# Attention and two feed-forward layers on one core: 288 bytes of padding, a shorter warm-up, and the odd slices of the last matmul tile by tile

## The chip, the cores and the metric

The kernel runs on one core of one Trainium2 chip. The metric is the device time of one execution in microseconds. [...]

## The reference

```python
scores = scale * np.matmul(q, k.transpose(0, 1, 3, 2))       # batch 4, heads 8, seq 576, head_dim 64
thresh = np.max(scores, axis=-1, keepdims=True) - tau
scores = np.where(scores >= thresh, scores, -1000000000.0)
scores = scores - np.max(scores, axis=-1, keepdims=True)
attn = np.exp(scores)
attn = attn / (np.sum(attn, axis=-1, keepdims=True) + 1e-09)
attn_out = np.matmul(attn, v)
x = np.ascontiguousarray(attn_out.transpose(0, 2, 1, 3)).reshape(B * S, H * D)   # 2304 x 512
h = x @ w_in                                                 # layer 1: 512 -> 2048
g = np.where(h >= 1, h, np.where(h <= -1, 0.0, (h + 1) ** 2 / 4))
x = g @ w_out                                                # 2048 -> 512
h = x @ w2_in                                                # layer 2: 512 -> 2048
r = np.maximum(h, 0.0)
out = (s * (r * r) + b) @ w2_out                             # 2304 x 512
```

## The kernel before

**A planner writes the order.** Every piece of work is handed to a list (`add`) with the engines that may do it, an estimate for each, a priority, and the data that it reads and writes. `Sched.run` then plays the list through in a model of its own and fixes the order on every engine; the program is issued in that order. So one changed piece can shift the order everywhere behind it. Where the model sees TensorE without work, it puts in a filler: a product of the identity matrix with itself into a free PSUM bank, which nobody reads (`fill`, L1397).

**Stages.** Attention comes first, head by head: scores on TensorE (L576 and L585), their minimum on VectorE (L631), the exponential on ScalarE (L634), the masking with the sum on VectorE (L639), normalising (L669, L674), transposes on TensorE (L695, L711), the product with the values (L733, L734). In its gaps, TensorE does the first eight of layer 1's sixteen slices of 128 hidden columns (L928, L961). Then follow three passes (`PASSES`): the rest of layer 1, and layer 2 in two halves of eight slices. Each pass takes three blocks of 768 tokens; in each block `gemm1` (L1223) makes eight slices of the hidden layer with seven products for each pair of slices, and a second matmul sums them with the output weights. An operand is kept as two float32r parts, high and low, so that a product is made of three matmuls: high times high, high times low, low times high.

**Layer 2's second matmul** (`gemm2`, L1299). A block has six tiles of 128 tokens, each with its own PSUM bank. The loaded operand is a slice of the hidden layer for 128 tokens (`G_b`), the streamed one 512 columns of output weights (`P.unit`). `rows` lists the slices in the order in which they get ready: 0, 2, 4, 6 (even), then 1, 3, 5, 7 (odd). When a bank is complete, VectorE adds it to the sum of the earlier pass (`joined`, L1131), or an engine copies it (`copied`), and SyncE's queue stores the tile (L1318).

**Where operands lie.** `lr` and `lh` are allocated from the left of a partition's bytes: `lr` starts at byte 17088, `lh` at 122560. The pools of the right side end at the top of the partition; the last of them, `final`, holds `pr` (starting at byte 163808) and behind it `pf`. `G_b` lies in `pr`, each slice 6144 bytes and its low part 3072 behind the high one, a tile's 128 columns every 512 bytes. The 44 units of weights, 2048 bytes each, lie in `lr` (36), `lh` (3) and `pr` (5, the low part of slice 3 and both parts of slices 5 and 7). Two of the slices, `G_b[5]` and `G_b[7]`, also take in turn the split input of the next block's `gemm1` (`ring`).

**The start.** `warm_up` makes the identity on GpSimd, copies it to `ident_r`, and issues 27 transposes of it on TensorE; the first heads' scores stand behind them in TensorE's order. The first operands `r0` to `r3` come by DMA and are scaled on ScalarE (L513) or GpSimd (L511) before the scores.

Of the kernel before, what the change touches and what calls it, by code (L numbers as in the profile page):

```python
# [7 lines left out]
F32 = mybir.dt.float32  # L8
# [24 lines left out]
NSX, NV = 4, 2  # L33

AHEAD = 1
WARM = 9

FILL = 200000.0
NE, NP, NST, NH, LEAD = 2, 3, 4, 3, 3
NYS = 8  # L40
CONV0 = 0.0
# [22 lines left out]
NJ = 4  # L64
# [19 lines left out]
O_EXTRA = 8 * BT * 2 * NJ  # L84
PR_BYTES = O_EXTRA + UNIT * (NPLACE - NLEFT - NTAIL - NFREE)
PF_BYTES = 8 * BT

# [35 lines left out]
class Sched:  # L125
# [72 lines left out]
    def run(self):  # L198
# [27 lines left out]
        while left:  # L226
# [22 lines left out]
            for e in engines:  # L249
# [51 lines left out]
                    break  # L301
                for item in held:
                    heapq.heappush(q, item)
                if e == "pe" and busy[e] <= now < self.fill_until:

                    b = next((b for b in self.fill_banks if bank_free.get(b, 0.0) <= now), None)
                    if b is not None:
                        t = Task()
                        t.alts, t.prio, t.idx, t.group, t.after = [], (9, 0), len(self.tasks) + seq, Group([(b,)]), 0.0
                        t.group.banks, t.group.left, t.succ, t.start = (b,), 1, [], now  # L310
                        t.fn = ("pe", self.fill_ns, self.fill(b))
                        bank_free[b] = HELD
                        busy[e] = array.run(now, self.fill_ns + self.CHANGE.get((self.kind, None), 0))
                        self.kind = None
                        self.burst = 0
                        order.append(t)
                        seq += 1
                        heapq.heappush(events, (busy[e], seq, t))
# [47 lines left out]
def attention_then_ffn(tc, qk, v, tau, w1, w2, s2, b2, out):  # L366
# [51 lines left out]
    garr = [xp_.tile([128, 2 * TM], F32R, name=f"g{i}") for i in range(NGL)]  # L418
    at_cm = tc.tile_pool(name="attn", bufs=1, side="right")
    ap_ = at_cm.__enter__()  # L420
    ident_r = ap_.tile([128, 128], F32R, name="identr")
    hs_b = [Buf("LF", 1280 * i, TM) for i in range(NH)]
    c_b = [Buf("LF", 3840 + 1280 * i, TM) for i in range(NH)]
    ye_b = [Buf("LF", 7680 + 1280 * i, TM) for i in range(2)]
# [39 lines left out]

    def consts():
        make_identity(nc, ident)
        nc.gpsimd.tensor_copy(out=ident_r, in_=ident)
        for c, x in ((half, 0.5), (part_c, 1.0 / S), (tiny_c, 1e-9)):
            nc.vector.memset(c, x)

# [304 lines left out]
    def warm_up():  # L775

        g = Group([(7,)])

        def mm():
            for _ in range(3 * WARM):  # L780
                nc.tensor.transpose(bank[7][:, 0:128].bitcast(F32R), ident_r, ident_r)

        add([("pool", 1260.0, consts)], (0, 0), w=["ident"])
        add([("pe", WARM * 213.0, mm)], (0, 0), r=["ident"], w=[("bank", g)], group=g)

# [23 lines left out]
    def final():  # L809
        late["md"].__exit__(None, None, None)  # L810
        xg.__exit__(None, None, None)
        late["cm"] = tc.tile_pool(name="final", bufs=1, side="right")
        q = late["cm"].__enter__()
        arena["PR"] = q.tile([128, PR_BYTES // 4], F32R, name="pr")
        arena["PF"] = q.tile([128, PF_BYTES // 4], F32, name="pf")

    def after(tasks, fn, key, r=()):
        sw = add([("host", 1, fn)], (0, aidx[0] + 1), r=r, w=[key])
# [234 lines left out]
    class Pass:  # L1053
# [6 lines left out]
        def product(self, p, j):  # L1060
            return ORDER.index(p) * self.nj + j
# [218 lines left out]
    def gemm2(P, t0, T):  # L1280

        if P.layer == 1:
            return gemm2_across(P, t0, T)

        m, n = T // 128, 512
        prs = [fresh() for _ in range(m)]
        ny = 6 + 4 * P.last
        gy = [(Group(ANY8), y_b[turn("y", ny)]) for _ in range(m)]
        rows = P.rows()

        def tokens(i):
            return slice(t0 + 128 * i, t0 + 128 * i + 128)

        def mm(f, i, g):
            o = bank[g.banks[0]][:, 0:n]
            wh, wl = (P.unit[P.out(f, y)](0, 512) for y in range(2))
            gh, gl = G_b[f](128 * i, 128), G_b[f](BT + 128 * i, 128)
            for s, (a, y) in enumerate(((gh, wh), (gh, wl), (gl, wh))):
                nc.tensor.matmul(o, a, y, start=(f == rows[0] and s == 0), stop=(f == rows[-1] and s == 2))  # L1299

        def sums(i):
            if P.n > 1 and i < m:
                y = gy[i][1]
                add([("sp", DMA_ISSUE, lambda: nc.sync.dma_start(out=y(), in_=yD[tokens(i), :]))], (0, prs[i][1][1] - 16),
                    r=[("yd", t0, i)], w=y.keys(), lag=128 * 4 * n)

        for i in range(ny):
            sums(i)
        for f in rows:
            for i in range(m):  # L1310
                ku = P.unit[P.out(f, 0)].keys() + P.unit[P.out(f, 1)].keys()
                kg = G_b[f].keys(128 * i, 128) + G_b[f].keys(BT + 128 * i, 128)
                product(prs[i][0], 3 * mm_ns(n), lambda f=f, i=i: mm(f, i, gy[i][0]), ku + kg, gy[i][0])
        for i in range(m):
            g, y = gy[i]
            po = prs[i][2]
            (joined if P.n > 1 else copied)(g, n, y, y.keys(), po)
            add([("sp", DMA_ISSUE, lambda y=y, i=i: nc.sync.dma_start(out=(out if P.last else yD)[tokens(i), :], in_=y()))], po,  # L1318
                r=y.keys(), w=[] if P.last else [("yd", t0, i)], lag=128 * 4 * n)
            sums(i + ny)  # L1320
# [150 lines left out]
```

## Time and profile before

| | |
|---|---|
| median of 3 runs | 1083.65 us (1081.87 to 1083.82) |
| time of the profiled execution | 1079.24 us |
| span of its profile | 1077.4 us |
| TensorE busy | 1052.1 us, 98% of the span, 6491 records |
| VectorE, ScalarE, GpSimd busy | 802.2, 704.6, 428.3 us |
| granted clock, mean | 1.0 |

The span reaches from the first to the last instruction that the profiler saw; 1.8 us of the time lie around it. A busy TensorE is not one at its peak, since ends of matmuls are modelled: the pace is read from start to start. A float32 product of the identity is two records.

### The profile page before, as it was taken

What the parts mean: (1) busy time and instruction counts of PE and PEld (TensorE: products, weight loads), DVE (VectorE), ACT (ScalarE), POOL (GpSimd) and SP (SyncE); (2) the same over time, 40 slices, a digit from 0 to 9 for tenths busy, and PEclk for the clock granted to TensorE, in tenths of its full rate; (3) what the DMA queues carried; (4) which work ended last, traced back from release to release, by engine and by line L of the source; (5) the groups of instructions that cost most, each with busy time, mean ns of one, the idle gap of its engine ahead of it and who ended that gap; (6) DMA issues with size and microseconds to landing.
All of it is one profiled execution on the core that took longest, in us unless ns stands there. A gap on an engine that the chain in (4) does not pass through costs nothing.

```text
span 1077.4 us, 19033 instructions
## 1 busy us (share of the span) xinstructions
PE 1052.1 (98%) x6491; PEld 925.3 (86%) x6491; DVE 802.2 (74%) x1596; ACT 704.6 (65%) x1322; POOL 428.3 (40%) x653
## 2 busy tenths in 40 slices
PE   9989999999999999999999999999999999999998
PEld 6556877788888898899999999998989889898996
DVE  7988998797887899757888979786796726356372
ACT  7998888898998988734535446265684626346260
POOL 5766767889898978332302111120100101000000
PEclk9999999999999999999999999999999999999999
DMA  5654455565647665599856499843638951140112
GB/s 169 201 156 148 137 184 193 187 199 174 184 137 217 182 198 169 188 355 365 297 173 224 129 307 348 309 168 131 230 128 279 343 174 63 40 137 20 60 30 87
DMA packets 105120, 199.95 MB, mean 186 GB/s; under 512 B 11328, under 2 KB 33344, under 8 KB 105024
## 3 DMA queue, kind: packets, MB, share of 16 engines
q1 hardware_dynamic: 105024, 198.75, 55.9%
q8 instruction: 51, 0.84, 0.3%
q14 instruction: 45, 0.37, 0.1%
HBM read 134.61 MB, written 64.09 MB: 184 GB/s over the span
## 4 chain that ended last, share of the span: by engine, by line
PE 71%; ACT 8%; DVE 6%; issue 2%; POOL 2%; DMA 1%; DVEq 0%; ACTq 0%; POOLq 0%
PE ps L1223 23%; PE ps L1299 18%; PE ps L1263 9%; PE ps L928 5%; PE ps L961 4%; PE ps L695 2%; PE ps L733 2%; PE ps L1009 2%; PE ps L585 2%; ACT p L674 2%; DVE p L639 1%; ACT e L634 1%; ACT pt L687 1%; PE ps L576 1%; PE ps L734 1%
## 5 line engine op out<-in xcount | busy, mean ns | idle before, releaser
L1223 PE MATMUL ps<-pr,lr 128*128 128x384 f32 x816 | 144.7, 336 | 0.0
L1223 PEld LDWEIGHTS ps<-pr,lr 128*128 128x128 f32 x816 | 141.7, 188 | 0.4 <-DVE lg L1131 0.2
L639 DVE SCALAR_TENSOR_TENSOR p<-ps,stt,e 128x576 f32<-128x576 f32 x144 | 116.3, 812 | 21.7 <-ACT e L634 16.8
L1223 PE MATMUL ps<-lr 128*128 128x384 f32 x672 | 122.2, 336 | 0.6 <-DVE lg L1131 0.3
L1223 PEld LDWEIGHTS ps<-lr 128*128 128x128 f32 x672 | 116.7, 188 | 3.1 <-issue 1.4
L631 DVE TENSOR_REDUCE stt<-ps 128x1 f32<-128x576 f32 x144 | 105.8, 749 | 18.2 <-PE ps L585 9.3
L928 PE MATMUL ps<-xh,lr 128*128 128x320 f32 (+1 forms) x512 | 112.6, 299 | 0.2 <-DVE lf L938 0.2
L634 ACT ACTIVATE e<-ps,stt 128x576 f32<-128x576 f32 x144 | 105.9, 751 | 10.4 <-DVE stt L631 9.9
L1299 PE MATMUL ps<-lr,pr 128*128 128x512 f32 x432 | 102.6, 397 | 0.2
L674 ACT ACTIVATE p<-p,stt 128x576 f32<-128x576 f32 (+3 forms) x112 | 93.3, 838 | 12.8 <-DVE stt L658 11.7
L555 DVE TENSOR_TENSOR pr<-lg,pr 128x768 fp32r<-128x768 f32 x71 | 69.2, 978 | 41.6 <-POOL pr L838 26.5
L1299 PEld LDWEIGHTS ps<-lr,pr 128*128 128x128 f32 x432 | 80.5, 188 | 21.0 <-DVE pf L1128 1.4
L1131 DVE TENSOR_TENSOR lg<-lg,ps 128x384 f32<-128x384 f32 (+1 forms) x104 | 56.3, 560 | 47.7 <-PE ps L1299 31.3
L695 PE MATMUL ps<-ident,p 128*128 128x128 f32 x576 | 82.7, 275 | 7.3 <-ACT pt L687 5.2
L928 PEld LDWEIGHTS ps<-xh,lr 128*128 128x128 f32 x512 | 85.1, 188 | 2.9 <-DVE lk L880 0.8
L961 PE MATMUL ps<-g,lr 128*128 128x256 f32 (+1 forms) x600 | 87.1, 297 | 0.0
L687 ACT COPY pt<-ps 128x512 f32<-128x512 f32 x143 | 79.9, 591 | 5.4 <-PE ps L695 5.1
L695 PEld LDWEIGHTS ps<-ident,p 128*128 128x128 f32 x576 | 66.0, 140 | 19.6 <-ACT pt L687 5.5
L1127 ACT COPY lg<-ps 128x384 f32<-128x384 f32 (+1 forms) x107 | 49.3, 494 | 50.8 <-PE ps L1223 44.2
L961 PEld LDWEIGHTS ps<-g,lr 128*128 128x128 f32 x600 | 80.7, 189 | 0.0
L928 PE MATMUL ps<-xl,lr 128*128 128x256 f32 (+1 forms) x256 | 75.3, 294 | 0.0
L733 PE MATMUL ps<-pt,vr 128*64 128x256 f32 (+1 forms) x512 | 69.1, 412 | 0.7 <-ACT pt L687 0.6
(128 smaller groups left out, 2268.1 us busy)
## 6 DMA issues: line engine op xcount, KB each, us to landing
wd<-lh SPq DMA_DIRECT2D x118, 256.0 KB, 4.0
lr<-wd SPq DMA_DIRECT2D x108, 256.0 KB, 5.5
lk<-in_w_dram SPq DMA_DIRECT2D x48, 512.0 KB, 4.5
vr<-in_v_dram SPq DMA_DIRECT2D x32, 320.0 KB, 3.4
r<-in_qk_dram SPq DMA_DIRECT2D x32, 288.0 KB, 3.1
lg<-y1T SPq DMA_DIRECT2D x6, 1536.0 KB, 7.4
lk<-in_w_dram SPq DMA_DIRECT2D x32, 256.0 KB, 3.8
r<-in_qk_dram SPq DMA_DIRECT2D x16, 304.0 KB, 4.2
```

Of the source, the lines that this page charges most:

```text
L631: add([("dve", 665, lambda: nc.vector.tensor_reduce(out=nm[:, x:x + 1], in_=Sv(), axis=AX.XY, op=ALU.min))], at(pr, "min"), r=[kg], w=[ks[ ...
L634: add([("act", 624, lambda: nc.scalar.activation(out=ev, in_=Sv(), func=AF.Exp, bias=nm[:, x:x + 1], scale=-1.0))], at(pr, "exp"), r=[kg, ...
L639: nc.vector.scalar_tensor_tensor(out=p[:, x * S:x * S + S].rearrange("p (a c) -> p a c", a=2), in0=Sv(), scalar=nthr[:, x:x + 1], in1=ev, ...
L674: nc.scalar.activation(out=p[i:j, o:o + w], in_=p[i:j, a:a + w], func=AF.Identity, scale=rc[i:j, x:x + 1], bias=un[i:j, x:x + 1])
L687: add([("act", actp_ns(n), lambda: [nc.scalar.copy(out=a, in_=b) for a, b in zip(dst, src())]), ("dve", dve_ns(n), lambda: [nc.vector.tens ...
L695: nc.tensor.transpose(bank[g.banks[0]][:, j * 128:(j + 1) * 128], p[:, c0 + j * 128:c0 + (j + 1) * 128], ident)
L733: nc.tensor.matmul(o[64 * x:64 * x + 64, 0:n], vr[:, c:c + D], PT[:, x, k, c0:c0 + n], start=(k == 0), stop=False)
L928: nc.tensor.matmul(o, a, x, start=(n == 0), stop=(n == 11))
L961: nc.tensor.matmul(o, a[:, c], x, start=(f == 0 and n == 0), stop=(f == nf - 1 and n == 2))
L1223: nc.tensor.matmul(o, a, y, start=(i == 0 and p in (1, 5, 2)), stop=(i == 5), skip_group_check=p not in (1, 5, 2))
L1263: nc.tensor.matmul(o, w, x, start=(f == rows[0] and s == 0), stop=(f == rows[-1] and s == 2))
L1299: nc.tensor.matmul(o, a, y, start=(f == rows[0] and s == 0), stop=(f == rows[-1] and s == 2))
```

## The change

`pf` gets 288 bytes more. The warm-up is five float32 products of the identity in place of 27 float32r transposes, and `ident_r` with its copy is gone. Fillers are allowed only from 4500 ns of the planner's time on. In `gemm2`, the even slices are still walked slice by slice over all tiles; the odd slices are walked tile by tile, all four for one tile before the next.

```diff
-WARM = 9
-
-FILL = 200000.0
+WARM = 5
+
+FILL_FROM, FILL = 4500.0, 200000.0
...
 PF_BYTES = 8 * BT
+PAD = 288
...
-                if e == "pe" and busy[e] <= now < self.fill_until:
+                if e == "pe" and FILL_FROM <= now and busy[e] <= now < self.fill_until:
...
-    ident_r = ap_.tile([128, 128], F32R, name="identr")
...
-        nc.gpsimd.tensor_copy(out=ident_r, in_=ident)
...
-            for _ in range(3 * WARM):
-                nc.tensor.transpose(bank[7][:, 0:128].bitcast(F32R), ident_r, ident_r)
+            for _ in range(WARM):
+                nc.tensor.matmul(bank[7][:, 0:128], ident, ident, start=True, stop=True)
...
-        arena["PF"] = q.tile([128, PF_BYTES // 4], F32, name="pf")
+        arena["PF"] = q.tile([128, (PF_BYTES + PAD) // 4], F32, name="pf")
...
-        for f in rows:
-            for i in range(m):
-                ku = P.unit[P.out(f, 0)].keys() + P.unit[P.out(f, 1)].keys()
-                kg = G_b[f].keys(128 * i, 128) + G_b[f].keys(BT + 128 * i, 128)
-                product(prs[i][0], 3 * mm_ns(n), lambda f=f, i=i: mm(f, i, gy[i][0]), ku + kg, gy[i][0])
+        walk = [(f, i) for f in rows[:NJ] for i in range(m)]
+        walk += [(f, i) for i in range(m) for f in rows[NJ:]] if True else [(f, i) for f in rows[NJ:] for i in range(m)]
+        for f, i in walk:
+            ku = P.unit[P.out(f, 0)].keys() + P.unit[P.out(f, 1)].keys()
+            kg = G_b[f].keys(128 * i, 128) + G_b[f].keys(BT + 128 * i, 128)
+            product(prs[i][0], 3 * mm_ns(n), lambda f=f, i=i: mm(f, i, gy[i][0]), ku + kg, gy[i][0])
```

TensorE at the start of the program, before (`r0` to `r3` are the heads' operands, `ps...` the PSUM banks, L576 the scores, L1397 a filler, L781 the warm-up; numbers behind a name are the program's own):

```order
L1397 MATMUL ps3_99<-ident_63 128x128 x4
L781 MATMUL ps3_99<-identr_86 128x128 x27
L1397 MATMUL ps3_99<-ident_63 128x128
L576 MATMUL ps2_0_92<-r0_111 128x288 x2
L1397 MATMUL ps3_99<-ident_63 128x128
L576 MATMUL ps2_1_93<-r1_112 128x288 x2
L576 MATMUL ps3_99<-r0_111 128x288 x2
L1397 MATMUL ps1_1_95<-ident_63 128x128 x5
L576 MATMUL ps2_0_92<-r1_112 128x288 x2
```

The same place of the changed kernel, whose lines stand one lower (L780 is the warm-up, L575 the scores):

```order
L780 MATMUL ps3_98<-ident_63 128x128 x5
L575 MATMUL ps2_0_91<-r0_110 128x288 x2
L575 MATMUL ps2_1_92<-r1_111 128x288 x2
L575 MATMUL ps3_98<-r0_110 128x288 x2
L1397 MATMUL ps1_1_94<-ident_63 128x128
L575 MATMUL ps2_0_91<-r1_111 128x288 x2
```

Fillers and transposes ahead of the first head are gone, and fewer fillers stand between the heads; in the whole program there are 46 after and 52 before, five of these ahead of the first head.

ScalarE at the start, before (L513 scales an operand, L634 is the exponential):

```order
L513 ACTIVATE r0_111<-r0_111 128x256
L513 ACTIVATE r1_112<-r1_112 128x256
L634 ACTIVATE e0_100<-ps2_0_92,stt0_105 128x576
L634 ACTIVATE e1_101<-ps2_1_93,stt0_105 128x576
L634 ACTIVATE e0_100<-ps3_99,stt1_106 128x576
```

And after (L512 and L633):

```order
L512 ACTIVATE r0_110<-r0_110 128x256
L512 ACTIVATE r1_111<-r1_111 128x256
L512 ACTIVATE r2_112<-r2_112 128x256
L633 ACTIVATE e0_99<-ps2_0_91,stt0_104 128x576
L633 ACTIVATE e1_100<-ps2_1_92,stt0_104 128x576
```

The scaling of the third operand, which GpSimd did before, now stands on ScalarE ahead of the first exponential.

TensorE at the end of the last block, before (the last two odd slices of the six tiles; `ps2_0` and `ps2_1` hold two tiles each, so that six products in a row belong to two tiles):

```order
L1299 MATMUL ps2_0_92<-pr_6011 128x512 x6
L1299 MATMUL ps2_1_93<-pr_6011 128x512 x6
L1299 MATMUL ps1_0_94<-pr_6011 128x512 x3
L1299 MATMUL ps1_1_95<-pr_6011 128x512 x3
L1299 MATMUL ps2_0_92<-pr_6011 128x512 x6
L1299 MATMUL ps2_1_93<-pr_6011 128x512 x6
L1299 MATMUL ps1_0_94<-pr_6011 128x512 x3
L1299 MATMUL ps1_1_95<-pr_6011 128x512 x3
```

And after (L1298; the last two tiles, four odd slices each):

```order
L1298 MATMUL ps1_0_93<-lh_69,pr_5957 128x512 x4
L1298 MATMUL ps1_0_93<-pr_5957 128x512
L1298 MATMUL ps1_0_93<-lh_69,pr_5957 128x512
L1298 MATMUL ps1_0_93<-pr_5957 128x512 x6
L1298 MATMUL ps1_1_94<-lh_69,pr_5957 128x512 x4
L1298 MATMUL ps1_1_94<-pr_5957 128x512
L1298 MATMUL ps1_1_94<-lh_69,pr_5957 128x512
L1298 MATMUL ps1_1_94<-pr_5957 128x512 x6
```

Twelve products in a row now complete one tile, where before each tile got its last three products within the last eighteen.

## Rows read from the trace of the kernel before

**Rows 1.** The page: span, then busy us, share, instructions of TensorE.
```profile
span 1077.4 us, 19033 instructions
PE 1052.1 (98%) x6491; PEld 925.3 (86%) x6491; DVE 802.2 (74%) x1596; ACT 704.6 (65%) x1322; POOL 428.3 (40%) x653
```

**Rows 2.** Busy us by stretch, with instructions, granted clock, DMA share, GB/s.
```profile
6.70:150.00 143.30, 135.91 (x948) 93.34 (x949) 132.10 (x347) 129.55 (x275) 99.30 (x197) 1.00 0.54 164
150.00:470.00 320.00, 311.00 (x2313) 270.62 (x2310) 262.29 (x620) 274.92 (x566) 253.71 (x371) 1.00 0.60 189
...
724.00:1073.00 349.00, 348.33 (x1707) 307.30 (x1705) 201.63 (x312) 178.49 (x274) 23.90 (x25) 1.00 0.38 130
```

**Rows 3.** Timeline of the start: start us, us, instruction, idle before it.
```profile
1.34 2.08 PE L1397 MATMUL ps<-ident 128*128 128x128 f32 x8 [1.34 <-POOL ident masks.py:199]
...
2.56 0.91 SPq L507 DMA_DIRECT2D r<-in_qk_dram  x2
...
3.39 0.42 ACT L513 ACTIVATE r<-r 128x256 f32<-128x256 f32 x1 [1.39 <-DMA r<-in_qk_dram]
...
5.60 0.42 ACT L513 ACTIVATE r<-r 128x256 f32<-128x256 f32 x1 [1.79 <-DMA r<-in_qk_dram]
...
6.70 0.76 PE L576 MATMUL ps<-r 64*128 64x288 f32 x4
...
8.97 1.38 PE L1397 MATMUL ps<-ident 128*128 128x128 f32 x10
...
9.28 0.81 DVE L639 SCALAR_TENSOR_TENSOR p<-ps,stt,e 128x576 f32<-128x576 f32 x1
```

**Rows 4.** Fillers (L1397) by stretch: busy us of TensorE and its loads.
```profile
6.70:20.00 13.30, 4.56 (x27) 3.35 (x26) 1.00 0.65 201
20.00:150.00 130.00, 11.13 (x68) 8.96 (x68) 1.00 0.53 160
150.00:470.00 320.00, 0.00 (x0) 0.00 (x0) 1.00 0.60 189
```

**Rows 5.** Timeline of TensorE, second matmul of the last block.
```profile
1039.20 17.03 PE L1299 MATMUL ps<-lr,pr 128*128 128x512 f32 x72
1056.06 4.60 PE L1299 MATMUL ps<-lh,pr 128*128 128x512 f32 x19
1060.50 0.39 PE L1299 MATMUL ps<-pr 128*128 128x512 f32 x1
...
1064.46 8.36 PE L1299 MATMUL ps<-pr 128*128 128x512 f32 x36
```

**Rows 6.** Source view of L1299: count, least/median/most ns, first and last start.
```profile
L1299 PE MATMUL ps<-lr,pr x432: 389/396/498, 724.2 to 1055.8; 128*128 128x512 f32 x144
...
L1299 PE MATMUL ps<-pr x252: 388/389/398, 745.8 to 1072.4; 128*128 128x512 f32 x126
...
L1299 PE MATMUL ps<-lh,pr x180: 392/396/397, 741.4 to 1064.2; 128*128 128x512 f32 x180
```

**Rows 7.** Groups by form, 384 columns: count, busy us, mean ns, idle before.
```profile
L1223 PE MATMUL ps<-pr,lr 128*128 128x384 f32 x816 | 144.7, 336 | 0.0
...
L1263 PE MATMUL ps<-pr,lr 128*128 128x384 f32 x288 | 51.1, 337 | 1.9 <-ACT pf L1127 1.9
...
L1263 PE MATMUL ps<-pr 128*128 128x384 f32 x168 | 33.0, 334 | 0.0
```

**Rows 8.** The end: VectorE's last additions, and landing of the last stores (L1318).
```profile
1072.70 1.28 DVE L1131 TENSOR_TENSOR lg<-lg,ps 128x512 f32<-128x512 f32 x2
...
DMA to landing us min/median/max: 2.0/2.1/2.4
```

**Rows 9.** Source view of the DMA issue at 2.56 us (L507).
```profile
DMA to landing us min/median/max: 4.6/4.6/4.6
```

**Rows 10.** Timeline of layer 2's first block: VectorE's last slice, TensorE's odd slices.
```profile
741.07 0.95 DVE L555 TENSOR_TENSOR pr<-pf,pr 128x768 fp32r<-128x768 f32 x1
...
741.36 4.60 PE L1299 MATMUL ps<-lh,pr 128*128 128x512 f32 x19
```

## The prediction

> **What bounds the kernel now.** I read the page first, then stretches, then the two places that the change touches. The page says that TensorE is busy for 1052.1 of 1077.4 us [rows 1], so the question is what TensorE does with its time. The stretches split it: up to 150 us it has 7.4 us idle in 143.3 us, from 150 to 470 us (attention with the first layer's products in the gaps) 9.0 us idle in 320, and from 724 to 1073 us (layer 2) 0.7 us idle in 349 [rows 2]. Not all of the busy time is work, though: the filling products on the identity matrix (L1397) take 4.56 us of the stretch from 6.7 to 20 us and 11.13 us of that from 20 to 150 us, and none stands after 150 us [rows 4]. So from 150 us on TensorE always has something that must be done, and a microsecond less of work, of filling or of a late start ends the program a microsecond sooner, as long as no new wait appears. The chain that ended last runs through TensorE to 1072.8 us, then through the last addition on VectorE and its store [rows 5, 8].
>
> **The pad.** It is the largest term. The pool that holds `pr` and `pf` ends at the top of the partition, so 288 bytes more in `pf` move both down by 288: `pr` from byte 163808 to 163520. `lr` stands at 17088 and `lh` at 122560, 103 x 1024 bytes apart. Before, `pr` lies 288 bytes off that grid; after, the three differ by multiples of 1024. In layer 2's second matmul (L1299) the loaded operand always lies in `pr`, the streamed one in `lr`, `lh` or `pr`. The last block shows the pace: 19 products that stream from `lh` take (4.60 - 0.39) / 18 = 233.6 ns from start to start, 72 from `lr` (1056.06 - 1039.20) / 72 = 234.2 with a short wait in it, and 36 where both lie in `pr` (8.36 - 0.39) / 35 = 227.7 [rows 5]. The medians of all blocks say the same, 396 against 389 ns [rows 6]. So with operands whose places differ by a multiple of 512 the chip takes 5.9 ns less, and 432 + 180 = 612 of the 864 products have the other relation [rows 5, 6]. If place is the cause: 612 x 5.9 = 3.6 us. Bounds: 0 if it is not, and 612 x 7 = 4.3 by the medians. I take 3.5, since the 252 are the same work on the same engine in the same blocks, right behind the others. For products of 384 columns I count nothing: L1263 has 337 against 334 ns, L1223 336 with operands in different buffers [rows 7], which bounds it at 408 x 3 = 1.2 us.
>
> [...]
>
> **The start.** Before, four fillers (eight records from 1.34 us), 27 transposes and one more filler stand ahead of the first head's scores, which start at 6.70, though its operand was scaled by 3.39 + 0.42 = 3.81 [rows 3]. After, five identity products end near 1.34 + 10 x 0.216 = 3.5 us, 0.216 being the spacing of those eight records. The first head can start near 3.9 and, at that half pace, end near 5.3. The second head's operand is scaled at 5.60 + 0.42 = 6.02 [rows 3], so TensorE goes on at about 6.1 with one head (0.7 us of work at full pace) done, where before it began at 6.70: 1.3 us ahead. VectorE is less far ahead. In the new ScalarE order the third operand's scaling stands before the first exponential; its DMA is issued at 2.56 and lands after 4.6 us [rows 3, 9], so scaling ends near 7.6, the exponential near 8.3, and the first masking starts near 8.45 instead of 9.28 [rows 3]: 0.8 us. I take 0.9, near the VectorE end, since VectorE is busy for 132.1 of the 143.3 us that follow [rows 2]. Fillers after this point are 46 in the new order, 47 in the old: two records of about 0.12 us, 0.2 us. Against it stands a colder TensorE. The identity products come 0.216 us apart at 1.34 and (1.38 - 0.28) / 9 = 0.12 at 8.97 [rows 3], so the engine ran at half pace first, although the granted-clock column prints 1.00 everywhere [rows 2]; the new start has gaps near 3.5 to 3.9 and 5.3 to 6.1, so full pace may come later. While VectorE sets the pace that costs little: 0 to 1.5 us, taken as 0.3. The removed copy `ident_r` (POOL, 0.3 us) delayed nothing but the transposes, and no other address moves with it.
>
> **Odd slices tile by tile.** The products are the same and so is their number; what moves is when each of the six tiles is complete. Before, all six become complete in the last 4 us, and VectorE's last two additions run to 1072.70 + 1.28 = 1073.98 behind a TensorE that ended at 1064.46 + 8.36 = 1072.82 [rows 5, 8]. After, tiles complete 12 x 0.23 = 2.8 us apart, so the last addition (0.68) can start at once: 1073.98 - 0.68 - 1072.85 = 0.45 us sooner, and its store travels alone, 2.0 instead of 2.4 us [rows 8]. Together 0.85 at most and 0 at least; I take 0.7. At the five other ends of a block TensorE does not wait now, so nothing is gained. Two things get tighter. Slice 7 is wanted in the first tile: in the tightest block it is ready at 741.07 + 0.95 = 742.0, and the walk of the odd slices starts at 741.36 [rows 10]; its third product, 11 products on, comes at 743.9, or 743.5 at the faster pace. That leaves 1.4 us. And `G_b[5]`, into which the next block splits its second operand, comes free some 0.7 us before the end instead of 4.1; cast and subtraction are two operations of about 0.95 [rows 10] and the first use comes after 24 products of 0.177 [rows 7], 4.2 us later: hidden by 3 us, and 1.9 us a block if it were not.
>
> **Sum.** 3.5 + 0.9 + 0.2 + 0.7 - 0.3 = 5.0 us. The profiled execution took 1079.24 us (span 1077.4), so 1074.2 by its measure. It lies 4.4 below the median of the runs shown, 1083.65, which I use for the forecast: **1078.6 us**. About 0.2% (2.2 us) is what a measurement of this kernel can tell from no change, so faster means below 1081.5.
>
> **Rivals.**
> - The pad does nothing, and place in `pr` was only a mark of something else, such as the late part of each block. For it: 384 columns show no difference, and the third odd slice, where records alternate between `lh` and `pr`, keeps a spacing of 0.23 [rows 5, 7]. Against it: the products with both operands in `pr` have 388, 389 and 398 ns as least, median and most over all six blocks, the others a median of 396 [rows 6]. 1083.65 - 1.5 = 1082.1: no change. [...]
> - The planner reorders the attention stage and the new interleaving is worse. Idle time up to 470 us is 16.4 us [rows 2] and fillers 15.7 [rows 4]; a tenth more of both is 3 us, giving 1081.6, at the edge of no change. As much better would give 1075.6.
> - The slow one: TensorE stays at half pace after the short warm-up. Place: 6 to 30 us. Price: from 6.7 to 20 us real work is 13.3 - 4.56 = 8.7 us at full pace [rows 4], 17.4 at half, 3.5 us more than the 13.9 us there are; later TensorE is needed about 86% of the time (135.9 less 15.7 and the first 8.7 in 130 us [rows 2, 4]), so half pace loses 0.36 us per us. The gain is gone if full pace comes at 25 us, and the kernel is slower by over 0.2% from 31 us on; at 35 us it gives about 1087. Against it: fillers start again as soon as TensorE has nothing to do. [...]
> - Slice 7 comes late in the first tile. A slip of s us costs s - 1.4 per block; VectorE's order there has changed. Slips of 3 us in two blocks give 1081.8.
>
> **How the numbers follow.** Forecast 0.62, pad without effect 0.12, worse interleaving 0.13 (half of it still faster), better 0.06, half pace 0.05, late slices 0.02. Faster 0.62 + 0.06 + 0.07 = 0.75, the same 0.12 + 0.06 + 0.01 = 0.19, slower 0.06. The range runs from the better interleaving with the upper bound of the pad, 1075.0, to the pad without effect, 1082.2; what is left out is most of the half pace, and the ends of the interleavings.
>
> **What would show it.** Pad: the medians of `lr,pr` and `lh,pr` fall to that of `pr` in the source view of the second matmul, and the layer-2 stretch of six blocks gets 3.5 us shorter. Start: first head before 4.5 us, first masking near 8.4, and a last filler about 1 us sooner. Tail: one addition and one store after the last product, 0.7 us less from there to the end. Wrong if 396 stays, if identity products are still 0.21 us apart after 15 us, or if TensorE waits at the start of an odd walk.

## The result and the profile after

The changed kernel takes 1093.83 us (median of 6 runs, 1092.2 to 1095.95), the kernel before 1082.76 us beside it (6 runs, 1081.0 to 1084.54). The ratio is 1.0105, 95% interval 1.0087 to 1.0123: slower by some 11 us. The forecast was 1078.6 us, the range 1075.0 to 1082.2: wrong in sign.

The two profiled executions stand further apart, 1095.88 against 1079.24 us. In half of the executions of the kernel before that ran beside the experiments (30 of 60), the mean granted clock, the share of TensorE's full speed that the profile prints, is under 0.999; their median is 1083.5 us, that of the others 1080.4. Below, medians of all runs stand with their ratios, and where kernels are added up, medians of the executions with a mean granted clock of at least 0.999 ("at full clock"): 1080.4 us for before, 1094.4 for after (five executions, 1092.2 to 1095.95).

The page of the kernel after (against [rows 1]) and its stretches (against [rows 2], with 470 to 724 us put in):

```profile
span 1094.1 us, 18937 instructions
PE 1055.1 (96%) x6462; PEld 922.8 (84%) x6462; DVE 802.7 (73%) x1580; ACT 707.9 (65%) x1321; POOL 442.1 (40%) x669
```

```profile
6.70:150.00 143.30, 135.16 (x912) 91.93 (x911) 128.46 (x323) 126.60 (x268) 95.88 (x197) 1.00 0.53 158
150.00:470.00 320.00, 312.62 (x2323) 270.46 (x2322) 264.77 (x629) 276.47 (x568) 253.73 (x371) 1.00 0.58 184
470.00:724.00 254.00, 248.67 (x1480) 245.46 (x1480) 195.37 (x306) 116.91 (x199) 58.40 (x55) 1.00 0.78 269
724.00:1073.00 349.00, 338.93 (x1675) 300.01 (x1674) 209.11 (x314) 185.77 (x286) 33.08 (x41) 1.00 0.40 135
```

TensorE's busy time is up by 3 us only; the span is up by 16.7. So the time is in waits: TensorE is idle for 10.1 us of the last stretch, where it was 0.7, and for 5.3 us of that from 470 to 724, where it was 2.5. The waits of TensorE from 720 us on (engine, line, what it waited for: us in total, times, longest) name them:

```profile
PE ps L1298 <- ACT pf L1126: 2.9, 5, 0.7
PE ps L1298 <- DVE lg L1130: 2.3, 3, 0.8
PE ps L1298 <- ACT lg L1126: 2.0, 3, 0.7
PE ps L1298 <- DVE lk L1130: 1.6, 2, 0.8
...
PE ps L1298 <- DVE pf L1130: 0.8, 1, 0.8
```

L1298 (L1299 before) is layer 2's second matmul; L1126 and L1130 are the copies and additions that empty its PSUM banks. The last block's timeline shows where in the walk they stand (against [rows 5]; TensorE, then VectorE):

```profile
1071.55 1.07 PE L1298 MATMUL ps<-lh,pr 128*128 128x512 f32 x4
...
1074.27 0.84 PE L1298 MATMUL ps<-lh,pr 128*128 128x512 f32 x3
1075.89 0.50 PE L1298 MATMUL ps<-lh,pr 128*128 128x512 f32 x1 [0.78 <-DVE lg L1130]
...
1080.78 0.84 PE L1298 MATMUL ps<-lh,pr 128*128 128x512 f32 x3
1082.41 0.50 PE L1298 MATMUL ps<-lh,pr 128*128 128x512 f32 x1 [0.78 <-DVE pf L1130]
...
1075.15 0.69 DVE L1130 TENSOR_TENSOR lg<-lg,ps 128x512 f32<-128x512 f32 x1 [4.69 <-PE ps L1298]
...
1090.22 0.69 DVE L1130 TENSOR_TENSOR lg<-lg,ps 128x512 f32<-128x512 f32 x1 [2.03 <-PE ps L1298]
```

Tile 0 is complete at 1074.3; three products of tile 1 run, then TensorE stands still until VectorE has added tile 0 (1075.15 + 0.69 = 1075.84). The same happens between tiles 2 and 3, and not between 1 and 2, 3 and 4, 4 and 5. In the first three blocks TensorE waits in the same places for ScalarE's copy of the tile, 0.68 to 0.73 us. A stall costs 1075.89 - 1074.27 - 3 x 0.227 = 0.94 us, and the first product behind it takes 0.33 us to the next instead of 0.23. Twice in each of six blocks, this makes the odd walk 18.0 to 18.2 us long, where it was 16.4 and where it is 16.1 with the pad alone (below). The end itself went as forecast (against [rows 8]): one addition of 0.69 us behind the last product, and 4.3 us from that product's start to the end of the span where it was 5.0.

The pad did what it was to do. The source view of L1298 (against [rows 6]) has the medians of `lr,pr` and `lh,pr` down from 396 to the 389 ns of `pr`:

```profile
L1298 PE MATMUL ps<-lr,pr x432: 387/389/500, 730.6 to 1071.3; 128*128 128x512 f32 x144
L1298 PE MATMUL ps<-pr x252: 387/389/398, 748.4 to 1089.8; 128*128 128x512 f32 x126
L1298 PE MATMUL ps<-lh,pr x180: 388/389/501, 747.5 to 1088.4; 128*128 128x512 f32 x180
```

The start (against [rows 3]; TensorE, then VectorE's first masking) did not:

```profile
1.34 2.50 PE L780 MATMUL ps<-ident 128*128 128x128 f32 x10 [1.34 <-POOL ident masks.py:199]
3.92 1.33 PE L575 MATMUL ps<-r 64*128 64x288 f32 x4
6.41 2.29 PE L575 MATMUL ps<-r 64*128 64x288 f32 x8 [1.16 <-ACT r L512]
8.63 0.79 PE L1397 MATMUL ps<-ident 128*128 128x128 f32 x2
...
14.96 0.79 PE L1397 MATMUL ps<-ident 128*128 128x128 f32 x2
...
16.31 0.61 PE L1397 MATMUL ps<-ident 128*128 128x128 f32 x4
...
9.01 0.82 DVE L638 SCALAR_TENSOR_TENSOR p<-ps,stt,e 128x576 f32<-128x576 f32 x1 [0.46 <-POOL r L510]
```

The fillers in the source views, before and after (count, least/median/most ns, first and last start):

```profile
L1397 PE MATMUL ps<-ident x104: 272/275/582, 1.3 to 147.7; 128*128 128x128 f32 x104
...
L1397 PE MATMUL ps<-ident x92: 273/275/581, 8.6 to 151.2; 128*128 128x128 f32 x92
```

The first head's scores start at 3.92 as forecast, but four of their products take 1.33 us where they took 0.76, and two identity records still take 0.79 us at 14.96, which the prediction named as a mark of being wrong; four take 0.61 at 16.31. In the trace's record of the granted clock the first entry, of 1.0, begins at 16.2 us; before, it began at 5.7. Below, "the full clock comes" means this entry. (Ahead of it the clock column prints 1.00 all the same, from 6.70 to 16.20 us too, so a late rise is not seen in the mean granted clock; it is seen in the pace, and so it is read in the runs below.) Two more of the prediction's marks fail: the first masking starts at 9.01 us, where 9.28 was the old time and 8.4 the forecast, and the last filler starts 3.5 us later instead of 1 us sooner. And the order behind the start is another one. Layer 1 pays for it, from its first products on:

```profile
507.27 0.70 PE L1008 MATMUL ps<-g,lr 128*128 128x320 f32 x3 [0.65 <-DVE md L1017]
...
525.00 3.22 PE L1222 MATMUL ps<-pr,lr 128*128 128x384 f32 x17 [1.23 <-DVE pr L554]
...
536.40 3.42 PE L1222 MATMUL ps<-lr 128*128 128x384 f32 x18 [1.43 <-DVE pf L1130]
```

For the experiments I divide each profile at three products: the first of layer 1's first matmul (L1223 before), the first and the last of layer 2's second. The lengths in us, in the order of the text:

| kernel | to layer 1 | layer 1 | layer 2 | end | time of the profiled execution | median at full clock |
|---|---|---|---|---|---|---|
| before | 503.0 | 221.2 | 348.2 | 5.0 | 1079.24 | 1080.4 (30 runs) |
| after | 505.4 | 225.2 | 359.2 | 4.3 | 1095.88 | 1094.4 (5) |
| pad alone | 507.0* | 220.8 | 344.2 | 5.0 | 1078.80 | 1074.7 (4) |
| walk alone | 504.8* | 222.8 | 361.0 | 4.3 | 1094.64 | 1092.9 (2) |
| start alone | 504.6 | 224.9 | 349.4 | 5.0 | 1085.70 | 1085.9 (7) |
| after, tiles apart | 505.2 | 224.4 | 347.1 | 4.3 | 1082.80 | 1082.3 (8) |
| pad and tiles apart | 506.0* | 220.8 | 344.7 | 4.3 | 1077.61 | 1074.7 (1) |
| five products, old order | 502.0 | 222.7 | 348.2 | 5.0 | 1079.69 | 1080.4 (5) |
| old warm-up, new order | 504.3* | 224.5 | 345.6 | 4.3 | 1080.51 | 1079.8 (6) |
| fillers from 0, tiles apart | 501.9 | 220.9 | 344.7 | 4.3 | 1073.63 | 1074.1 (4) |
| six products, tiles apart | 504.5 | 220.7 | 344.8 | 4.3 | 1076.07 | 1076.4 (4) |

*: in this execution the mean granted clock is 0.996 (pad alone, pad and tiles apart) or 0.998 (walk alone; old warm-up, new order). With the pad alone it fell to 0.50 for 6.8 us from 68.4 us on, with the old warm-up for 3.4 us from 11.8.

### The profile page after: what moved, and what is told of

It reads as the page before. It is cut to its first block, busy times and chain, and to the rows that moved or that the text cites. A ratio compares the mean times of both kernels' runs of the same rounds, so it can differ in the third digit from the quotient of the medians.

```text
span 1094.1 us, 18937 instructions
## 1 busy us (share of the span) xinstructions
PE 1055.1 (96%) x6462; PEld 922.8 (84%) x6462; DVE 802.7 (73%) x1580; ACT 707.9 (65%) x1321; POOL 442.1 (40%) x669
## 4 chain that ended last, share of the span: by engine, by line
PE 67%; ACT 14%; DVE 11%; issue 3%; POOL 2%; DMA 2%; SPq 0%; DVEq 0%; ACTq 0%; POOLq 0%
PE ps L1222 19%; PE ps L1298 18%; PE ps L1262 9%; PE ps L960 4%; PE ps L927 4%; ACT p L673 3%; ACT e L633 3%; DVE p L638 3%; PE ps L732 3%; PE ps L694 2%; PE ps L575 2%; ACT pt L686 2%; PE ps L1008 2%; DVE stt L630 1%; DVE lg L1130 1%
## 5 line engine op out<-in xcount | busy, mean ns | idle before, releaser
L630 DVE TENSOR_REDUCE stt<-ps 128x1 f32<-128x576 f32 x144 | 106.0, 747 | 16.1 <-PE ps L575 11.2
L633 ACT ACTIVATE e<-ps,stt 128x576 f32<-128x576 f32 x144 | 105.2, 745 | 6.9 <-DVE stt L630 3.5
L1126 ACT COPY lg<-ps 128x384 f32<-128x384 f32 (+1 forms) x111 | 51.6, 494 | 81.9 <-PE ps L1222 57.2
L673 ACT ACTIVATE p<-p,stt 128x576 f32<-128x576 f32 (+3 forms) x116 | 95.7, 827 | 13.4 <-DVE stt L657 12.3
L1298 PE MATMUL ps<-lr,pr 128*128 128x512 f32 x432 | 100.3, 391 | 1.4 <-ACT pf L1126 0.9
L1298 PEld LDWEIGHTS ps<-lr,pr 128*128 128x128 f32 x432 | 80.3, 188 | 20.2 <-ACT pf L1126 1.7
L1130 DVE TENSOR_TENSOR lg<-lg,ps 128x384 f32<-128x384 f32 (+1 forms) x104 | 56.4, 558 | 37.1 <-PE ps L1298 21.5
```

What stands on the lines that cost most here:

```text
L630: add([("dve", 665, lambda: nc.vector.tensor_reduce(out=nm[:, x:x + 1], in_=Sv(), axis=AX.XY, op=ALU.min))], at(pr, "min"), r=[kg], w=[ks[ ...
L633: add([("act", 624, lambda: nc.scalar.activation(out=ev, in_=Sv(), func=AF.Exp, bias=nm[:, x:x + 1], scale=-1.0))], at(pr, "exp"), r=[kg, ...
L673: nc.scalar.activation(out=p[i:j, o:o + w], in_=p[i:j, a:a + w], func=AF.Identity, scale=rc[i:j, x:x + 1], bias=un[i:j, x:x + 1])
```

## The experiments

**The pad alone.** The kernel before with

```diff
+PAD = 288
...
-        arena["PF"] = q.tile([128, PF_BYTES // 4], F32, name="pf")
+        arena["PF"] = q.tile([128, (PF_BYTES + PAD) // 4], F32, name="pf")
```

> The kernel before with the 288 bytes alone; the order of all instructions is that of the kernel before. If the relative place of streamed and loaded operand in the partition sets the pace of the 512-column products, 612 of them take 5.9 ns less each: medians of lr,pr and lh,pr in the second matmul of layer 2 at 389 instead of 396 ns, and 3.4 to 3.6 us less in all (ratio near 0.9968). If place is only a mark of something else, medians stay at 396 ns and the ratio at 1.000.

1074.81 us, ratio 0.9941 (0.9921 to 0.9961). Layer 2 is 4.0 us shorter in the profile. The source view of its second matmul:

```profile
L1300 PE MATMUL ps<-lr,pr x432: 387/389/504, 727.8 to 1055.7; 128*128 128x512 f32 x144
L1300 PE MATMUL ps<-pr x252: 388/389/389, 748.8 to 1072.0; 128*128 128x512 f32 x126
L1300 PE MATMUL ps<-lh,pr x180: 389/389/389, 744.5 to 1063.8; 128*128 128x512 f32 x180
```

Every instruction stands in the same order as before, on all engines. Place is the cause, and the pad is worth a little more than the theory's 3.5 us: 4.0 in layer 2 and 0.4 in layer 1. The medians at full clock say 5.7; see what stays open, below.

**The walk alone.** The kernel before with the odd slices of `gemm2` tile by tile:

```diff
-        for f in rows:
-            for i in range(m):
...
+        walk = [(f, i) for f in rows[:NJ] for i in range(m)]
+        walk += [(f, i) for i in range(m) for f in rows[NJ:]] if True else [(f, i) for f in rows[NJ:] for i in range(m)]
+        for f, i in walk:
...
```

> The kernel before with the odd slices tile by tile, nothing else. Theory: two token tiles share one two-bank PSUM buffer, and waits are kept for the buffer, so the first product of the second tile in it that comes after the first tile's last product waits for VectorE's or ScalarE's eviction of the first. Two such waits of 0.7 us with some 0.2 us of restart in each of six blocks, less 0.7 us at the end: +9 to +10 us, 1092 to 1093 us, and twelve idle stretches of about 0.7 us in the odd walks. Rival: the walk costs nothing and the new start and its replanned order are the cause: -0.7 to 0 us and no such stretches.

1093.79 us, ratio 1.0107 (1.0086 to 1.0129). Layer 2 takes 12.8 us more and the end 0.7 less. The last block stands still in the same two places:

```profile
1072.84 0.85 PE L1299 MATMUL ps<-lh,pr 128*128 128x512 f32 x3
1074.47 0.50 PE L1299 MATMUL ps<-lh,pr 128*128 128x512 f32 x1 [0.78 <-DVE lg L1131]
...
1081.07 0.50 PE L1299 MATMUL ps<-lh,pr 128*128 128x512 f32 x1 [0.78 <-DVE pf L1131]
```

The walk by itself explains the size of the whole loss.

**The start alone.** The kernel before with

```diff
-WARM = 9
-
-FILL = 200000.0
+WARM = 5
+
+FILL_FROM, FILL = 4500.0, 200000.0
...
-                if e == "pe" and busy[e] <= now < self.fill_until:
+                if e == "pe" and FILL_FROM <= now and busy[e] <= now < self.fill_until:
...
-            for _ in range(3 * WARM):
-                nc.tensor.transpose(bank[7][:, 0:128].bitcast(F32R), ident_r, ident_r)
+            for _ in range(WARM):
+                nc.tensor.matmul(bank[7][:, 0:128], ident, ident, start=True, stop=True)
```

and without `ident_r`.

> The kernel before with the new start alone: five identity products on the float32 identity, no ident_r, fillers only from the planner's 4.5 us on. Theory: granted full clock comes at about 16 instead of 6 us and costs some 2.4 us, and the replanned order adds waits in layer 1 worth up to 3.5 us: +3 to +6 us, ratio 1.003 to 1.006. Rival (the prediction's): the start is 0.9 us ahead and the clock costs 0.3 us: ratio 0.999 to 1.000.

1086.09 us, ratio 1.0036 (1.0022 to 1.005); 5.5 us at full clock. The stretch to layer 1 is 1.6 us longer, layer 1 is 3.7 longer with the waits that the kernel after has, layer 2 is 1.2 longer:

```profile
524.17 3.22 PE L1221 MATMUL ps<-pr,lr 128*128 128x384 f32 x17 [1.24 <-DVE pr L553]
...
535.56 3.40 PE L1221 MATMUL ps<-lr 128*128 128x384 f32 x18 [1.42 <-DVE pf L1129]
```

The prediction's start (0.9 and 0.2 less 0.3, 0.8 us of gain) is refuted. What the late clock costs and what the order costs is left to the runs below.

**After, with the tiles apart.** The kernel after with one line changed:

```diff
-        walk += [(f, i) for i in range(m) for f in rows[NJ:]] if True else [(f, i) for f in rows[NJ:] for i in range(m)]
+        walk += [(f, i) for i in (0, 2, 4, 1, 3, 5) for f in rows[NJ:]]
```

> The kernel after with the odd slices still tile by tile, but the tiles in the order 0, 2, 4, 1, 3, 5: the same products, and no two tiles of one PSUM buffer next to each other. If the shared buffer is what TensorE waits for, the twelve idle stretches go and the time falls by 10 to 11 us against the kernel after, to about 1083 us. If walking tile by tile is slow in itself (late odd slices, alternation of lh and pr), it stays near 1093 us.

1082.25 us, ratio 1.0 (0.9987 to 1.0013) to before, 11.6 us under the kernel after. TensorE's waits from 720 us on lose those for evictions in the odd walk; the waits that are left stand ahead of it:

```profile
PE ps L1222 <- DVE lg L1130: 1.1, 2, 0.6
PE ps L1298 <- ACT pf L1126: 0.9, 2, 0.6
PE ps L1222 <- DVE pf L1130: 0.5, 1, 0.5
...
```

Against the kernel after, VectorE's order differs in 10 places and ScalarE's in 12, so this is hardly another plan. So walking tile by tile is not slow in itself. What is slow is that two tiles of one PSUM buffer follow each other.

**Pad and tiles apart.** The kernel before with the pad and the walk of the last run, and the old start.

> The kernel before with the pad and the odd slices tile by tile in the tile order 0, 2, 4, 1, 3, 5; the start is the old one. If the three parts add up, it is the pad alone (1074.8 us at an undisturbed clock) less the 0.7 us of the shorter end: 1074.1 us, ratio near 0.993. If the shared buffer still costs a wait between tiles that don't follow each other, or the walk moves waits into the next block, it is at 1076 us or more.

1077.55 us, ratio 0.996 (0.9943 to 0.9978): in six of the seven executions the mean granted clock is under 0.999, and the seventh took 1074.71 us. In the profile the parts add up: layer 1 220.8, layer 2 344.7 (0.5 us more than with the pad alone), end 4.3. Against the run before this one, the new start costs 3.6 us in layer 1 and 2.4 in layer 2.

**Five products, old order.** In the kernel before, the 27 transposes are replaced when they are issued; the planner still reckons with them, so that no other instruction moves:

```diff
-            for _ in range(3 * WARM):
-                nc.tensor.transpose(bank[7][:, 0:128].bitcast(F32R), ident_r, ident_r)
+            for _ in range(5):
+                nc.tensor.matmul(bank[7][:, 0:128], ident, ident, start=True, stop=True)
```

> The kernel before in its own order of instructions, but with five identity products on the float32 identity issued in place of the 27 transposes; nothing else differs, so no later instruction changes its place. If the loss of the new start is the late full clock, the granted clock rises at 15 us or later, and it is 1 to 2.5 us slower than before (1083.5 to 1085). If the loss is the replanned order, this kernel has none of it: -0.5 to +0.3 us, and the stretch of layer 1 keeps its length in both cases.

1081.4 us, ratio 0.9996 (0.9983 to 1.0009). The run does not do what I wanted of it: the full clock came at 4.7 us, earlier than before (the ten records of the five products start 0.18 us apart on average from 3.21 us on, the eight of the fillers ahead of them 0.23). Here the four fillers of the old order still stand ahead of the five products, and no pause follows. But it tells that the five products as such don't delay the clock here, and layer 1 is reached 1.0 us sooner, about what the prediction gave for the start. The profile loses that again in one wait of 1.60 us at 592 us for an addition of VectorE; the profile of the walk alone has it too (in each of the two, layer 1's products wait 1.9 us in two waits for that addition), those of the kernel before and of all the kernels with a pad haven't. It stays unexplained.

**Old warm-up, new order.** The kernel with the tiles apart, in which four identity products and the 27 transposes are issued in place of the five products; `ident_r` and its copy are there again, and the planner knows nothing of it:

```diff
...
-            for _ in range(WARM):
+            for _ in range(4):
                 nc.tensor.matmul(bank[7][:, 0:128], ident, ident, start=True, stop=True)
+            for _ in range(27):
+                nc.tensor.transpose(bank[7][:, 0:128].bitcast(F32R), ident_r, ident_r)
```

> The kernel of the run with the tiles apart (new start, new order of instructions, pad), with four identity products and the 27 transposes issued in place of the five products; the order of everything else is kept. If the late clock is the loss, the clock rises near 6 us and the time falls by 1 to 2.5 us to about 1080. If the replanned order is the loss, layer 1 keeps its 224 us with the waits of TensorE for VectorE near 523 and 535 us, and the time stays within 0.7 us of 1082.3.

1080.4 us, ratio 0.9993 (0.998 to 1.0007). At full clock it is 2.5 us under the kernel with the tiles apart (1079.8 against 1082.3), though its first head starts at 6.17 us and not at 4.10. The full clock is there by then (twelve score products from 6.17 us take 1.73 us, where eight from 6.41 us took 2.29 in the kernel after), but in the profiled execution the granted clock fell to 0.50 from 11.8 to 15.2. In the two profiles, 0.9 us of the difference stand ahead of layer 1, less than without that fall, and 1.5 in layer 2, where both have the full clock. So the late clock costs some 0.9 us or more, and that all of the 2.5 is its price is not shown. Layer 1 keeps its 224.5 us, and the kernel is 5.1 us above pad and tiles apart (1074.7, one run): that is the order.

**Fillers from 0, tiles apart.** The kernel with the tiles apart and one number changed:

```diff
-FILL_FROM, FILL = 4500.0, 200000.0
+FILL_FROM, FILL = 0.0, 200000.0
```

> The kernel of the run with the tiles apart (pad, five identity products, no ident_r) with FILL_FROM at 0, so that fillers may stand beside the warm-up again. The order of all engines is then that of the kernel before with pad and tiles apart, but for four more fillers and the five products in place of the 27 transposes. If keeping fillers out of the first 4.5 us is what both delayed the full clock and led the planner to the other order, the clock rises near 5 us, layer 1 takes 221 instead of 224.5 us, and the time is 1074 to 1075 us at an undisturbed clock, 1077 with one dip (ratio 0.993 to 0.996). If the short warm-up itself is at fault, it stays near 1082.

1074.37 us, ratio 0.9945 (0.9927 to 0.9962), the fastest of all. The full clock comes at 4.4 us (the ten records of the five products start 0.17 us apart on average from 3.21 us on, the eight of the fillers ahead of them 0.23), the order is the old one (VectorE's and ScalarE's instructions stand exactly as with pad and tiles apart), and the beginning of layer 1 has none of the waits:

```profile
6.12 0.76 PE L575 MATMUL ps<-r 64*128 64x288 f32 x4
...
501.94 4.33 PE L1222 MATMUL ps<-lr 128*128 128x384 f32 x24
506.10 4.32 PE L1222 MATMUL ps<-lh,lr 128*128 128x384 f32 x24
510.26 8.83 PE L1222 MATMUL ps<-lr 128*128 128x384 f32 x48
...
527.25 4.52 PE L1222 MATMUL ps<-lr 128*128 128x384 f32 x24
```

So neither the five products nor the lost `ident_r` cost anything, and the early first head is not needed: here it starts at 6.12 us, 2.2 later than in the kernel after. The bound of 4500 ns on the fillers did: it kept the identity products from going on, and it gave the planner another order.

**Six products, tiles apart.** The kernel with the tiles apart and `WARM = 6`; the fillers are still kept out until 4500 ns.

> The kernel of the run with the tiles apart with six identity products in place of five, fillers still only from 4.5 us on. The planner, told 213 ns more, gives another order (663 rows of TensorE stand otherwise than in the kernel before, against 756). If the order behind the new start is bad by accident of the planning, layer 1's stretch changes by a microsecond or more either way, and the full clock still comes at about 15 us. If the loss in layer 1 follows from the short start as such, it stays at 224 to 225 us and the time at 1082.

1077.22 us, ratio 0.9966 (0.9952 to 0.9981). Layer 1 takes 220.7 us, so the loss there came from one particular order, not from a short start. Against my expectation the full clock came early as well, at 4.7 us, within four score products that take 0.99 us, where the kernel after took 1.33 and, at its full clock, 0.76:

```profile
1.34 2.93 PE L780 MATMUL ps<-ident 128*128 128x128 f32 x12 [1.34 <-POOL ident masks.py:199]
4.20 0.99 PE L575 MATMUL ps<-r 64*128 64x288 f32 x4
6.27 1.24 PE L575 MATMUL ps<-r 64*128 64x288 f32 x8 [1.09 <-ACT r L512]
```

Here the identity products go on to 4.3 us and the first head follows; with five they end at 3.8, the head follows within 0.3 us in all three profiles, and the full clock comes at 14.7 to 16.2 us. Why one product more decides it the runs don't tell. The order with six has a price of its own: layer 1 is reached at 504.5 us, 2.6 later than with fillers from 0.

**Other pads.** The kernel before with `PAD` = 32, 256 and 96, one execution each. They put `pr` 256, 32 and 192 bytes off the grid of `lr` and `lh`; before it was 288, with the pad of the change 0.

> The kernel before with a pad of 32 bytes in place of 288, so that the loaded operand in pr stands 256 bytes off the 1024-byte grid of lr and lh. If any place off the grid is slow, products streamed from lr and lh stay at 233 ns from start to start and layer 2's six blocks at 348.2 us; if 256 bytes count as aligned, 227 ns and 344.3 us.

> The kernel before with a pad of 256 bytes: pr stands 32 bytes off the 1024-byte grid of lr and lh. If what counts is whether the two operands' places differ by a multiple of 64 bytes (288 did not, 0 and 256 do), it is as slow as before, 234 ns from start to start, layer 2's six blocks 348.2 us, about 1079 us. If nearness to the grid counts, 227 ns and 344.1 us.

> The kernel before with a pad of 96 bytes: pr stands 192 bytes off the grid, a multiple of 64 but not of 128. If 64 is the step that counts, 227 ns and layer 2 in 344.1 us, about 1074.5 us; if the step is 128 or 256, 234 ns and 348.2 us, about 1079 us.

32 takes 1074.51 us, 256 takes 1083.09, 96 takes 1080.2 (in the latter two the mean granted clock is 0.997; with 96 it fell to 0.50 for 6.8 us). Layer 2's six blocks take 344.1, 348.2 and 345.8 us. The group of `lr,pr` in the source views, in this order:

```profile
L1300 PE MATMUL ps<-lr,pr x432: 387/389/502, 723.6 to 1051.3; 128*128 128x512 f32 x144
```

```profile
L1300 PE MATMUL ps<-lr,pr x432: 389/396/503, 728.1 to 1059.7; 128*128 128x512 f32 x144
```

```profile
L1300 PE MATMUL ps<-lr,pr x432: 388/392/505, 727.6 to 1056.9; 128*128 128x512 f32 x144
```

Three levels: 389 ns with a difference of 0 or 256 bytes, 392 with 192, 396 with 32 or 288. Products with both operands in `pr` have a median of 389 ns at every pad, so it is not the place of `pr` by itself. Neither of the two theories had a middle level.

## Why the prediction was wrong

**The odd slices: the step that failed.** "At the five other ends of a block TensorE does not wait now, so nothing is gained. Two things get tighter." I priced the end of the program (right: 4.3 instead of 5.0 us from the last product on) and looked for what gets tighter in slice 7 and `G_b[5]` (neither came late). I did not ask what the next product behind a finished tile has to wait for. The rows of the order that I showed say that six products in a row to `ps2_0` belong to two tiles; so do twelve and twelve in the new walk. Its end, with waits (TensorE; the last product of tile 0, then tile 1):

```
2661 L1298 MATMUL ps2_0_91<-pr_5957 128x512 [waits DVE_49]
2662 L1298 MATMUL ps2_0_91<-lh_69,pr_5957 128x512 x3
2663 L1298 MATMUL ps2_0_91<-lh_69,pr_5957 128x512 [waits DVE_49]
2664 L1298 MATMUL ps2_0_91<-pr_5957 128x512
```

The program's waits go by the buffer, not by its two banks. The three products of tile 1 that are issued ahead of tile 0's addition pass; the fourth waits until the addition is done, although it writes the other bank. In the old walk the tiles' ends came all together at the end of the block, behind the last product into either bank. Price: the predicted -0.7 us became +11 to +12 us, from twelve stalls of 1.0 us (0.94 and the slow restart) less the 0.7. The walk alone (+11.3 by medians, +12.5 at full clock) and tiles apart (-11.6 against after) agree from both sides. These tiles have banks of their own; the trace shows 0.78 us of idle all the same, where two banks are one buffer for the program.

**The start: wrong in sign.** "I take 0.9", less the 0.3 for the colder TensorE, plus 0.2 for fillers: 0.8 us of gain became 3.6 us of loss by the medians and 5.5 at full clock. The first head did start at 3.92 us, but that head start bought little: the first masking came at 9.01 us, not at 8.45, since the third operand's scaling ended at 8.26 and not near 7.6. The rival "half pace after the short warm-up", to which I gave 0.05, happened until 16 us (four score products take 1.33 us at 13.70 and 0.76 at 17.41). I took 0.3 us for it and 1.5 as the bound; the old warm-up in the new order gives 0.9 or more ahead of layer 1 and 2.5 in the whole time, so whether the bound held stays open. I argued that "fillers start again as soon as TensorE has nothing to do"; the first one comes at 8.63 us, as the rows of the start show, and that a filler brings the full pace was my estimate. The larger part, some 5 us with the tiles apart, is the planner's order, and 3.7 of it (224.5 against 220.8 in layer 1) fell due 500 us later than where I looked: the rival "worse interleaving" bounded itself to the time up to 470 us.

**The pad: right, and somewhat undersized.** 3.5 us forecast, with 4.3 as the bound by medians. One quotient of the sum was slightly off: (4.60 - 0.39) / 18 is 233.9 ns and not 233.6, which makes 6.2 ns a product and 3.8 us. Layer 2 shows 4.0 (pad of 288) and 4.1 (pad of 32), layer 1 another 0.4, which I had counted as nothing. The rival that place is no cause is refuted: only addresses moved. The runs show 4 us in layer 2, whose second matmul has 512 columns, and 0.4 in layer 1, whose products have 384. The sentence "operands whose places differ by a multiple of 512" was too narrow: 256 bytes are as good (a median of 389 ns).

**The ladder.** At full clock: before 1080.4, pad 1074.7, tiles apart on top 1074.7 (one run), new start on top 1082.3, tiles adjacent 1094.4. So the measured +14.0 is -5.7 for the pad, 0 for the end by a single run (-0.7 in the profile), +7.6 for the start and +12.1 for the shared buffers. By the medians of all runs the whole is +11.1. The start costs 2 us more here than alone (+5.5); layer 2 has 2.4 us more waits there and only 1.2 alone.

**What stays open.** The pad is worth 5.7 us in medians at full clock and 4.4 in the profiles' stretches. The kernel before spreads over 1079.1 to 1082.3 us at full clock, the pad alone over 1074.5 to 1074.8; the wait of 1.60 us at 592, which shows in two of four profiles without a pad and in none of those with one, would fit, but nothing here shows its cause. Open, too, is why one identity product, six in place of five, decides when the full clock comes, and what makes up the 1.5 us in layer 2 between the two kernels that differ in the warm-up alone.

## What to carry to other kernels

Before work is regrouped so that results are finished one by one, look at which finished result shares a buffer (as the program counts buffers, not banks) with the next one: here each such neighbour made TensorE wait 0.68 to 0.78 us for the eviction, and an order of the tiles that separates them took the wait away. Where a planner writes the order, a changed start is a new order for the whole program: it is to be judged by the stretches far behind it, and tested by issuing the new work in the old order and the old work in the new. And the relative place of the operands that one matmul streams and loads is worth a try; here 32 bytes of padding were worth as much as 288, with 389 ns a product in place of 396.

## What the hardware showed unexpectedly

**Relative place of the operands.** The profiles' median of a 512-column product is 389 ns (some 227 from start to start) where streamed and loaded operand differ by 0 or 256 bytes (and multiples of 512), 392 at 192, and 396 (some 234 before) at 32 and 288. Layer 1, whose products have 384 columns, takes 220.8 us at 0 and 221.2 at 288 (without the wait at 592 us), in single profiles; the median of `gemm1`'s 816 products with operands in `pr` and `lr` is 334 ns at 0 and 336 at 288. Other differences were not tried.

**The granted clock at the start and later.** The full clock came at 4.4 us with fillers from 0, at 4.7 with five products in the old order and with six products, at 5.7 before, and by 6.17 with the old warm-up in the new order: in all of these, identity products or transposes went on to 4.3 us or later. In the three profiles in which five products ended at 3.8, it came at 14.7 to 16.2 us (two identity records take 0.49 us at 14.81 with the start alone, and 0.79 at 14.96 in the kernel after). The mean granted clock is under 0.999 in 30 of 60 executions of the kernel before, and in 4 of 24 of the three kernels with the late rise; in the profile of the kernel after, TensorE has no gap over 0.23 us from 59 to 80 us. With the pad alone:

```profile
20.00:68.40 48.40, 42.24 (x289) 25.54 (x289) 45.08 (x123) 44.54 (x93) 33.75 (x69) 1.00 0.57 169
68.40:75.20 6.80, 6.55 (x28) 3.19 (x29) 4.77 (x13) 5.85 (x14) 2.59 (x7) 0.50 0.34 98
75.20:150.00 74.80, 73.46 (x518) 54.59 (x517) 66.79 (x175) 65.54 (x144) 51.31 (x97) 1.00 0.51 152
```

Around the fall TensorE was idle twice, waiting for ScalarE: for 0.82 and 0.25 us up to 68.17 and 68.75. The kernel before has the same two gaps, up to 67.37 and 67.95 us, in its profile, and its clock did not fall there; what makes it fall is not shown. The price is some 3 us an execution (medians 1083.5 against 1080.4 us).
